# VectorE's and ScalarE's work on the quads as a loop with waits on registers, and PSUM banks of its own for the last quad

## The chip, the cores and the metric

The kernel runs on one core of a Trainium2 chip. The core has five engines, each with its own instruction stream: TensorE (PE in the profile), VectorE (DVE), ScalarE (ACT), GpSimd (POOL) and SyncE (SP), which issues most of the loads. They meet only at semaphores. The metric is the device time of one execution in microseconds, the median of several runs. All times below are in microseconds unless marked otherwise.

## What is computed

Attention for one new token of each of 32 sequences, over the last 512 positions of the key and value caches, with 32 query heads that share 8 key/value heads, and a projection on either side:

```python
B, Sq, D = 32, 1, 512
Hq, Hkv, Sk, Dh = 32, 8, 2048, 128
W = 512                                  # the window: the last 512 positions
q = (x @ wq).reshape(B, Sq, Hq, Dh).transpose(0, 2, 1, 3)
k = jnp.repeat(k_cache[:, :, Sk - W:, :], 4, axis=1)
v = jnp.repeat(v_cache[:, :, Sk - W:, :], 4, axis=1)
scores = jnp.einsum("bhqd,bhkd->bhqk", q, k) * (Dh ** -0.5)
p = softmax(scores, axis=-1)
o = jnp.einsum("bhqk,bhkd->bhqd", p, v)
out = o.transpose(0, 2, 1, 3).reshape(B, Sq, Hq * Dh) @ wo
```

Everything is bfloat16. The two windows are 33.5 MB each, wq and wo 4 MB each, so some 75.5 MB have to come from memory.

## The kernel before

**Quads.** The 32 sequences are worked on in eight quads of four, q = 0 to 7. The keys of a quad are one load K(q) of 4 MB (a partition holds 128 positions of one sequence, head and quarter of the window), its values one load V(q) of 4 MB, from quad 5 on in two pieces V(q).0 and V(q).1. There are two buffers for keys and two for values, used in turn. wo comes last, in three pieces W0 to W2, into the first key buffer.

**The steps of a quad**, with the letter that stands for each in the hand-written orders:

- T(q).0, T(q).1: VectorE transposes one half of the quad's keys each (line 516).
- S(q).0, S(q).1: TensorE multiplies each half with the queries, into the PSUM bank S_ps (line 346).
- M(q): VectorE takes the row maxima and their negative (lines 522 and 524).
- X(q): ScalarE's exponential, which also sums (line 565).
- N(q): VectorE's reciprocal and product, the weights in bfloat16 (lines 528 and 530).
- E(q): TensorE moves the weights to the rows on which the values lie, into EP_ps (line 360).
- G(q): ScalarE copies them out of PSUM into PTc (line 572).
- B(q): the weights are spread over a block-diagonal operand bd, heads 0 to 3 by VectorE (line 536), 4 to 7 by ScalarE (line 578).
- P(q): TensorE's weighted sum of the values, 32 groups of four products (line 372), into the four banks O_ps; P(q).a.b is groups a to b.
- C(q): the four pieces of the sum are copied to SBUF, by VectorE (line 541), ScalarE (line 583) or both.
- F(q): TensorE folds them into the layout that the output product wants (line 382), into F_ps; D(q): ScalarE stores the fold in o_sel (line 586).

After the last D, TensorE multiplies o_sel with wo (line 467), VectorE and ScalarE copy the result out (lines 550 and 597), and two stores end the kernel.

**What sets the order.** Every engine executes its instructions in the order in which they stand. TensorE's order is a head, three passes of a hardware loop over two quads (BODY_OPS), and a tail. VectorE's and ScalarE's orders are hand-written lists of all eight quads, DVE_OPS and ACT_OPS, without a loop; in VectorE's list the transposes of quads 6 and 7 stand ahead of steps of the quads before. `needs` gives what each step waits for, and ends in waits on constants. SP issues the loads in the order of LOADS: K(q) waits for T(q-2).1, V(q) for P(q-2) or the part of it that frees the piece, W0 to W2 for T6.1. A load that waits holds back all that stand behind it.

**PSUM.** The eight banks are S_ps, EP_ps, four of O_ps, F_ps and Y_ps (the output product). P(q) waits for the copies C(q-1), as all quads use the same four banks.

**Before the quads.** x is transposed by products, multiplied with wq into all eight banks (line 334), copied to SBUF in pieces of 512 columns by VectorE (line 505) and ScalarE (line 559) in turn, and the queries are transposed (line 508).

The loads, the orders and the loop's waits in the code:

```python
LOADS = """
K0 K1 V0.0 K2 V1.0 K3 V2.0 K4 V3.0 K5 K6 V4.0 K7 V5.0 V5.1 V6.0 V6.1 V7.0 V7.1 W0 W1 W2
""".split()
V_PIECES = 5 * [[0, 32]] + 2 * [[0, 16, 32]] + [[0, 18, 32]]
```

Of the kernel before, what the change touches and what calls it, by code (L numbers as in the profile page):

```python
# [19 lines left out]
S0.0 S0.1 S1.0 S1.1 E0 E1 P0.0.32  # L20
# [6 lines left out]
P7.0.18 P7.18.32 F6 F7  # L27
"""
ROUNDS = 3
DVE_OPS = """  # L30
T0.0 T0.1 T1.0 M0 T1.1 N0 M1 N1 B0.0.4 B1.0.4 T2.0 T2.1 M2 N2 B2.0.4 T3.0 T3.1 M3 N3 B3.0.4 T4.0
T4.1 M4 N4 B4.0.4 T5.0 C3.2.3 T5.1 C3.3.4 T6.0 M5 T6.1 N5 B5.0.4 C4.2.4 M6 T7.0 N6 T7.1 B6.0.4
C5.2.4 M7 N7 B7.0.5 C6.2.4 C7.2.4
"""
ACT_OPS = """
X0 X1 G0 B0.4.8 G1 B1.4.8 C0.0.4 X2 D0 G2 B2.4.8 C1.0.4 X3 D1 G3 B3.4.8 C2.0.4 X4 D2 G4 B4.4.8
C3.0.2 X5 D3 G5 B5.4.8 C4.0.2 X6 D4 G6 B6.4.8 C5.0.2 X7 D5 G7 B7.5.8 C6.0.2 C7.0.2 D6 D7
"""
# [14 lines left out]
def bass_standalone__sliding_block_cached__sampling_kernel(  # L53
# [22 lines left out]
    NG = 4  # L76
# [7 lines left out]
    orders = {"PE": head + sum(rounds, []) + tail, "DVE": ops_of(DVE_OPS), "ACT": ops_of(ACT_OPS)}  # L84

    ends, total = {}, {}
    for eng, ops in orders.items():
        for op in ops:
            kind = op[0]
            key = ("ANY", "C") if kind == "C" else (eng, kind)  # L90
            total[key] = total.get(key, 0) + (op[3] - op[2] if kind == "C" else 1)
            if kind == "C":
                ends["C", op[1]] = key + (4 * op[1] + 4,)
            elif kind == "B":
                for i in range(op[2], op[3]):
                    ends[kind, op[1], i] = key + (total[key],)
            elif kind == "P":
                for g in range(op[2], op[3]):
                    ends["P", op[1], g] = key + (total[key],)
            elif kind == "D":  # L100
                ends[op] = key + (total[key] + 1,)
            else:
                ends[op] = key + (total[key],)

    def needs(op):
# [3 lines left out]
        if kind == "T":  # L109
            d = [("S", q - 1, op[2])]  # L110
        elif kind == "S":
            d = [("T", q, op[2]), ("X", q - 1)]
        elif kind == "M":
            d = [("S", q, 1)]
        elif kind == "X":
            d = [("M", q), ("N", q - 1)]
        elif kind == "N":
            d = [("X", q), ("E", q - 1)]
        elif kind == "E":
            d = [("N", q), ("G", q - 1)]  # L120
        elif kind == "G":
            d = [("E", q)] + spread(q - NG)
        elif kind == "B":
            d = [("G", q), ("P", q - 2, 31)]
        elif kind == "P":
            d = spread(q) + [("C", q - 1)]
        elif kind == "C":
            d = [("P", q, 31), ("F", q - 2)]
        elif kind == "F":
            d = [("C", q)]  # L130
        elif kind == "D":
            d = [("F", q)]
        return [ends[n] for n in d if n[1] >= 0]

    with ExitStack() as es:
# [3 lines left out]
        K_sb = [sb(f"K_sb{i}", [P, R * DH], BF16) for i in range(2)]  # L139
# [9 lines left out]
        PTc = sb("PTc", [P, NG, R, REP], BF16)  # L149
        C_sb = sb("C_sb", [P, 2, 4, DH], F32)  # L150
        o_sel = sb("o_sel", [P, NI, B], BF16)
# [3 lines left out]
        maxv = sb("maxv", [P, NQ], F32)  # L155
        negmax = sb("negmax", [P, NQ], F32)
        sums = sb("sums", [P, NQ], F32)
        recip = sb("recip", [P, NQ], F32)
# [10 lines left out]
        F_id = spare[:, 1280:1536].bitcast(F32).rearrange("p (r h) -> p r h", r=4)  # L169
        m_id = spare[:, 1536:1792].bitcast(F32).rearrange("p (b h k) -> p b h k", b=4, h=HKV)  # L170
        F_hd = spare[:, 1792:1856].bitcast(F32)
        m_red = spare[:, 1856:1920].bitcast(F32)
# [7 lines left out]
        S_ps, EP_ps, O_ps, F_ps, Y_ps = ps[:, 0], ps[:, 1], ps[:, 2:6], ps[:, 6], ps[:, 7]  # L180

        def folds(q):
            return (F_ps if q < NQ - 1 else S_ps)[:, 0:4 * NI]
# [57 lines left out]
        def _(sp):  # L241
# [3 lines left out]
            for op in ops_of(" ".join(LOADS)):  # L245
                kind, q = op[0], op[1]
                if kind == "K":
                    if q >= 2:
# [23 lines left out]
        def _(pool):  # L272
# [10 lines left out]
            pool.sem_inc(op_sem["ACT", "D"], 1)  # L283
# [3 lines left out]
            diag(F_id[:, :, :], [[-32, 4], [-1, HQ]], "pool_f")  # L287
            diag(m_id[:, :, :, :], [[-32, 4], [-4, HKV], [-1, KB]], "pool_m")
# [30 lines left out]
        def _(pe):  # L319
# [48 lines left out]
            def pv(q, g0, g1):  # L368
                for g in range(g0, g1):
                    for b in range(4):  # L370
                        pr = slice(32 * b, 32 * b + 32)
                        ins = pe.matmul(  # L372
                            O_ps[:, b, :],
# [6 lines left out]
            def fold(q):  # L380
                for d in range(4):
# [3 lines left out]
                        rhs=C_sb[:, q % 2, :, NI * d:NI * d + NI],  # L385
# [11 lines left out]
            def waits_of(op):  # L397
# [3 lines left out]
                if kind == "S" and op[2] == 0:  # L401
                    yield ("ONE", "pool_qbd"), 4 * (q // 2) + 4
                    if q == 0:
                        yield ("ONE", "dve_q"), 4
                        yield ("ONE", "act_q"), 4
                elif kind == "E" and q == 0:
                    yield ("ONE", "pool_e"), 2
                elif kind == "F" and q < NQ - 1:
# [51 lines left out]
            for j, (i0, i1) in enumerate(WOP):  # L460
                pe.wait_ge(sem_wo[j], 16)
                last = j == len(WOP) - 1
                for cs in ((0, 1), (2, 3)) if last else (range(4),):
                    for i in range(i0, i1):
                        for c in cs:
# [3 lines left out]
                                lhsT=o_sel[:, i, :],  # L469
# [6 lines left out]
        def spread_args(q, h):  # L476
            return bd[:, q % 2, :, h, :], PTc[:, q % NG], mask[:, h:h + 1]

        def pick_args(q, r):
            pr = slice(32 * r, 32 * r + 32)  # L480
            return C_sb[pr, q % 2], O_ps[pr, :, r * DH:(r + 1) * DH]

        @block.vector
        def _(dve):
            wait = Waits(dve)
# [5 lines left out]
            dve.tensor_reduce(  # L491
                F_hd[:, :], F_id[:, :, :].rearrange("p r h -> p h r"), AX.X, ALU.add
            ).then_inc(s["dve_c"], 1)
            dve.wait_ge(s["pool_m"], 2)
            dve.tensor_reduce(
                m_red[:, :].rearrange("p (h k) -> p h k", h=HKV),
                m_id[:, :, :, :].rearrange("p b h k -> p h k b"), AX.X, ALU.add,
            ).then_inc(s["dve_c"], 1)
            dve.wait_ge(s["dve_c"], 2)
            dve.tensor_reduce(  # L500
                mask[:, :], m_red[:, :].rearrange("p (h k) -> p h k", h=HKV), AX.X, ALU.add
            ).then_inc(s["dve_c"], 1)
            for n in range(4):
                dve.wait_ge(s["pe_q"], 2 * n + 1)
                dve.tensor_copy(Q_row[:, 1024 * n:1024 * n + 512], ps[:, 2 * n]).then_inc(s["dve_q"], 1)  # L505
            dve.wait_ge(s["dve_q"], 4)
            dve.wait_ge(s["act_q"], 4)
# [6 lines left out]
            def turn(q, w):  # L514
                dve.wait_ge(sem_k[q % 2], 16 * (q // 2 + 1))
                return dve.transpose(  # L516
                    KT_sb[:, w].bitcast(F32).rearrange("p r c t -> p r (c t)"),
                    K_sb[q % 2][:, :].bitcast(F32).rearrange("p (r w c) -> p r w c", r=R, w=2)[:, :, w],
                )

            def maxes(q):
                dve.tensor_reduce(maxv[:, q:q + 1], S_ps, AX.X, ALU.max).then_inc(s["dve_m"], 1)  # L522
                dve.wait_ge(s["dve_m"], q + 1)
                return dve.tensor_scalar(  # L524
                    negmax[:, q:q + 1], maxv[:, q:q + 1], -SCALE, None, op0=ALU.mult)

            def norm(q):
                dve.reciprocal(recip[:, q:q + 1], sums[:, q:q + 1]).then_inc(s["dve_r"], 1)
                dve.wait_ge(s["dve_r"], q + 1)
                return dve.tensor_scalar(  # L530
                    P_bf[:, :], P_f32[:, :], recip[:, q:q + 1], None, op0=ALU.mult)

            def spread(q, h0, h1):
                for h in range(h0, h1):
                    o, i, m = spread_args(q, h)
                    ins = dve.tensor_scalar(o, i, m, None, op0=ALU.mult)  # L536
                return ins

            def pick(q, r0, r1):
                for r in range(r0, r1):  # L540
# [89 lines left out]
```

## Time and profile before

| | us |
|---|---|
| median of 3 runs (183.39 to 183.97) | 183.55 |
| the profiled execution | 183.87 |
| its span, first to last instruction | 182.6 |
| TensorE busy | 118.9 (65%) |
| VectorE busy | 105.8 (58%) |
| ScalarE busy | 49.7 (27%) |
| GpSimd busy | 12.4 (7%) |
| 16 transposes of keys on VectorE, 4.43 each | 70.5 |
| moved: 75.70 MB, mean 415 GB/s | |

The page cuts the span into 40 slices of 4.6 us and gives the busy share of each engine and of the 16 DMA engines in tenths; PEclk is the clock that TensorE was granted, in tenths of full speed (mean 0.822). The chain is followed back from the last instruction, at each step to what released it. A timeline lists instructions in order of time: start, duration, engine, line, operation, what it writes and reads, and how often, and in brackets the idle time before it with what ended it. An engine whose idle time nobody waits for costs nothing.

### The profile page before, as it was taken

Reading aid. Unit: us, or ns where it says so; the run is one execution under the profiler, and the core shown is the slowest. Engines: PE = TensorE matmul, PEld = TensorE weight load, DVE = VectorE, ACT = ScalarE, POOL = GpSimd, SP = SyncE. Lnnn points to the kernel's source line nnn. Section 1 sums busy time; section 2 is a strip of 40 time slices with the busy share of each in tenths; the row PEclk is TensorE's granted clock in tenths of the full one; section 3 lists DMA queues with packets and bytes.
Section 4 is the critical chain, followed back from the end, with each engine's and each line's share of the span. In section 5 each row is a group of like instructions: output and inputs, shape, how many; then the busy total and the mean of one; then the engine's idle time right before and its main releaser. Section 6 shows DMA issues by size and latency. Waiting matters only on the chain.

```text
span 182.6 us, 3659 instructions
## 1 busy us (share of the span) xinstructions
PE 118.9 (65%) x1636; PEld 57.6 (32%) x1636; DVE 105.8 (58%) x101; ACT 49.7 (27%) x92; POOL 12.4 (7%) x34
## 2 busy tenths in 40 slices
PE   0029901425869898049954899334299869996984
PEld 0013300101535353015521453003035434552553
DVE  0031499999559713983279317999902799633030
ACT  3001300000490527402470107100106406443031
POOL 7400012000300000003000000003000000000000
PEclk9999995555769999756995589755559999999999
DMA  6999999999999999999999999999999999999991
GB/s 235 461 431 409 424 459 438 431 395 460 449 431 388 449 456 416 395 452 449 425 398 438 438 447 409 431 438 445 424 416 416 427 424 438 416 436 437 424 374 56
DMA packets 3461, 75.70 MB, mean 415 GB/s; under 512 B 412, under 2 KB 508, under 8 KB 636
## 3 DMA queue, kind: packets, MB, share of 16 engines
q1 hardware_dynamic: 3360, 75.52, 96.7%
q8 instruction: 7, 0.11, 0.3%
q10 hardware_dynamic: 92, 0.05, 0.1%
q14 instruction: 2, 0.02, 0.0%
HBM read 75.53 MB, written 0.03 MB: 414 GB/s over the span
## 4 chain that ended last, share of the span: by engine, by line
DMA 39%; PE 28%; DVE 25%; ACT 3%; issue 3%; SPq 0%; DVEq 0%
DVE KT_sb L516 20%; DMA K_sb<-in_k_cache_dram 16%; DMA V_sb<-in_v_cache_dram 16%; PE ps L372 16%; DMA V_sb<-in_wq_dram 7%; PE ps L334 5%; PE ps L346 3%; DVE QT_sb L508 2%; PE ps L360 2%; ACT bd L578 1%; PE ps L382 1%; DVE C_sb L541 1%; PE ps L467 1%; DVE maxv L522 1%; DVE bd L536 1%
## 5 line engine op out<-in xcount | busy, mean ns | idle before, releaser
L516 DVE STREAM_TRANSPOSE KT_sb<-K_sb 128x4096 f32<-128x4096 f32 x16 | 70.5, 4429 | 4.6 <-DMA K_sb<-in_k_cache_dram 4.5
L372 PE MATMUL ps<-V_sb,bd 32*128 32x512 bf16 x1024 | 62.7, 398 | 9.6 <-DMA V_sb<-in_v_cache_dram 6.5
L346 PE MATMUL ps<-KT_sb,QBD 128*32 128x512 bf16 x256 | 24.6, 527 | 36.2 <-DVE KT_sb L516 32.1
L372 PEld LDWEIGHTS ps<-V_sb,bd 32*128 32x128 bf16 x1024 | 27.0, 97 | 40.5 <-issue 9.8
L346 PEld LDWEIGHTS ps<-KT_sb,QBD 128*32 128x32 bf16 x256 | 6.6, 113 | 52.4 <-DVE KT_sb L516 35.4
L536 DVE TENSOR_SCALAR bd<-PTc,mask 128x512 bf16<-128x512 bf16 x33 | 9.4, 349 | 22.5 <-ACT PTc L572 22.5
L565 ACT ACTIVATE P_f<-ps,negmax 128x512 f32<-128x512 f32 x8 | 5.5, 689 | 58.0 <-DVE negmax L524 58.0
L578 ACT ACTIVATE bd<-PTc,mask 128x512 bf16<-128x512 bf16 x31 | 19.9, 712 | 0.3
L583 ACT ACTIVATE C_sb<-ps 32x512 f32<-32x512 f32 x22 | 13.0, 589 | 21.7 <-PE ps L372 21.4
L541 DVE COPY C_sb<-ps 32x512 f32<-32x512 f32 x10 | 6.9, 693 | 12.9 <-PE ps L372 12.7
L312 POOL COPY QBD<-QT_sb 32x256 bf16<-32x256 bf16 x16 | 6.3, 396 | 106.0 <-PE ps L346 91.2
L572 ACT ACTIVATE PTc<-ps 128x512 bf16<-128x512 f32 x8 | 4.8, 595 | 27.9 <-PE ps L360 27.9
L382 PE MATMUL ps<-C_sb,F_pad 128*128 128x128 f32 x64 | 12.0, 345 | 0.4 <-DVE C_sb L541 0.4
L382 PEld LDWEIGHTS ps<-C_sb,F_pad 128*128 128x128 f32 x64 | 10.2, 242 | 4.8 <-issue 2.9
L360 PE MATMUL ps<-P_bf,E_sb 128*128 128x128 bf16 x128 | 9.5, 233 | 2.2 <-DVE P_bf L530 2.2
L334 PE MATMUL ps<-V_sb,bd 128*128 128x512 bf16 x32 | 9.2, 459 | 1.9 <-DMA V_sb<-in_wq_dram 1.9
L360 PEld LDWEIGHTS ps<-P_bf,E_sb 128*128 128x128 bf16 x128 | 8.1, 105 | 6.3 <-issue 3.4
L522 DVE TENSOR_REDUCE maxv<-ps 128x1 f32<-128x512 f32 x8 | 5.5, 687 | 7.5 <-PE ps L346 7.5
L323 PE MATMUL ps<-bd 32*128 32x128 bf16 x4 | 0.6, 294 | 10.6 <-DMA bd<-in_x_dram 10.6
L487 DVE CAST bd<-ps 128x512 bf16<-128x512 f32 x1 | 0.7, 691 | 11.3 <-PE ps L323 11.3
L559 ACT ACTIVATE KT_sb<-ps 128x512 bf16<-128x512 f32 x4 | 2.4, 598 | 17.1 <-PE ps L334 17.1
L505 DVE CAST KT_sb<-ps 128x512 bf16<-128x512 f32 x4 | 2.8, 692 | 6.7 <-PE ps L334 6.7
(29 smaller groups left out, 31.0 us busy)
## 6 DMA issues: line engine op xcount, KB each, us to landing
K_sb<-in_k_cache_dram SPq DMA_DIRECT2D x8, 4096.0 KB, 24.6
V_sb<-in_v_cache_dram SPq DMA_DIRECT2D x5, 4096.0 KB, 29.4
V_sb<-in_v_cache_dram SPq DMA_DIRECT2D x4, 2048.0 KB, 21.0
V_sb<-in_wq_dram SPq DMA_DIRECT2D x1, 4096.0 KB, 12.3
K_sb<-in_wo_dram SPq DMA_DIRECT2D x1, 2816.0 KB, 20.9
V_sb<-in_v_cache_dram SPq DMA_DIRECT2D x1, 2304.0 KB, 13.1
V_sb<-in_v_cache_dram SPq DMA_DIRECT2D x1, 1792.0 KB, 14.8
K_sb<-in_wo_dram SPq DMA_DIRECT2D x1, 1024.0 KB, 22.7
```

Source lines behind the costliest of these rows:

```text
L312: pool.tensor_copy(QBD[pr].rearrange("p u a (h c) -> p u a h c", h=HKV).rearrange("p u (w t) h c -> p (u w) t h c", w=2)[:, :, :, :, 4 * b ...
L334: ins = pe.matmul(ps[:, n], lhsT=xT_sb[:, kt, :], rhs=wq_sb[:, kt, n * 512:(n + 1) * 512], start=kt == 0, stop=kt == DKT - 1, tile_positio ...
L346: ins = pe.matmul(S_ps[32 * c:32 * c + 32, :], lhsT=QBD[:, q % 2, 2 * w + t, c0:c0 + 32], rhs=KT_sb[:, w, :, KB * h:KB * h + KB, t], start ...
L360: ins = pe.matmul(EP_ps[:, e * R:(e + 1) * R], lhsT=window[:, KB - 1 - k:KB - 1 - k + P], rhs=P_bf[:, k * R:(k + 1) * R], start=k == 0, st ...
L372: ins = pe.matmul(O_ps[:, b, :], lhsT=bd[pr, q % 2, 4 * g:4 * g + 4].rearrange("p r h e -> p (r h e)"), rhs=V_sb[q % 2][pr, 512 * g:512 * ...
L382: ins = pe.matmul(folds(q), lhsT=F_sb[:, d].rearrange("p h d -> p (h d)"), rhs=C_sb[:, q % 2, :, NI * d:NI * d + NI], start=d == 0, stop=d ...
L516: return dve.transpose(KT_sb[:, w].bitcast(F32).rearrange("p r c t -> p r (c t)"), K_sb[q % 2][:, :].bitcast(F32).rearrange("p (r w c) -> ...
L522: dve.tensor_reduce(maxv[:, q:q + 1], S_ps, AX.X, ALU.max).then_inc(s["dve_m"], 1)
L536: ins = dve.tensor_scalar(o, i, m, None, op0=ALU.mult)
L541: dve.tensor_copy(*pick_args(q, r)).then_inc(op_sem["ANY", "C"], 1)
L578: ins = act.activation(o, i, ACTF.Copy, scale=m)
L583: act.activation(*pick_args(q, r), ACTF.Copy).then_inc(op_sem["ANY", "C"], 1)
```

## The change

The lists DVE_OPS and ACT_OPS go. VectorE's and ScalarE's steps are hardware loops over n = 0 to 7. VectorE's turn n is T(n).0, T(n).1, then (from n = 2) its half of C(n-2), then M(n), N(n), B(n); ScalarE's is X(n), then (from n = 2) D(n-2), then G(n), its half of B(n), then (from n = 1) its half of C(n-1). What is left over of quads 6 and 7 stands behind the loops. Semaphore levels that depend on n are computed into registers; a branch on n being odd chooses the key buffer. SP increments some semaphores ahead of K2 by constants (BIAS), so that levels are a multiple of n plus a positive number.

TensorE keeps its loop and its body; its head now has E0 ahead of S1, and P0 in four pieces with E1 between them; its tail has P7 in four pieces. All PSUM banks are renumbered, and P(7) goes to the four upper banks (those of S_ps, EP_ps, F_ps and Y_ps), so it waits for D(5) instead of C(6); F(6) and F(7) go to the two lowest banks. C_sb has one buffer for quads 0 to 6 and one for quad 7. PTc and the small statistics have one buffer instead of four or eight. The queries are copied in two pieces of 1024 columns per engine instead of four of 512, and the mask is reduced in one step instead of two. The order of the loads and what they wait for is unchanged.

```diff
 HEAD_OPS = """
-S0.0 S0.1 S1.0 S1.1 E0 E1 P0.0.32
+S0.0 S0.1 E0 S1.0 S1.1 P0.0.12 E1 P0.12.16 P0.16.20 P0.20.32
 """
 TAIL_OPS = """
-P7.0.18 P7.18.32 F6 F7
+P7.0.12 P7.12.16 P7.16.18 P7.18.32 F6 F7
 """
-DVE_OPS = """
-T0.0 T0.1 T1.0 M0 T1.1 N0 M1 N1 B0.0.4 B1.0.4 T2.0 T2.1 M2 N2 B2.0.4 T3.0 T3.1 M3 N3 B3.0.4 T4.0
-T4.1 M4 N4 B4.0.4 T5.0 C3.2.3 T5.1 C3.3.4 T6.0 M5 T6.1 N5 B5.0.4 C4.2.4 M6 T7.0 N6 T7.1 B6.0.4
-C5.2.4 M7 N7 B7.0.5 C6.2.4 C7.2.4
-"""
-ACT_OPS = """
-X0 X1 G0 B0.4.8 G1 B1.4.8 C0.0.4 X2 D0 G2 B2.4.8 C1.0.4 X3 D1 G3 B3.4.8 C2.0.4 X4 D2 G4 B4.4.8
-C3.0.2 X5 D3 G5 B5.4.8 C4.0.2 X6 D4 G6 B6.4.8 C5.0.2 X7 D5 G7 B7.5.8 C6.0.2 C7.0.2 D6 D7
-"""
...
         elif kind == "P":
-            d = spread(q) + [("C", q - 1)]
+            d = spread(q) + [("C", q - 1) if q < LAST else ("D", q - 2)]
...
-        PTc = sb("PTc", [P, NG, R, REP], BF16)
+        PTc = sb("PTc", [P, R, REP], BF16)
...
-        S_ps, EP_ps, O_ps, F_ps, Y_ps = ps[:, 0], ps[:, 1], ps[:, 2:6], ps[:, 6], ps[:, 7]
+        O_ps, S_ps, EP_ps, F_ps, Y_ps = ps[:, 0:4], ps[:, 4], ps[:, 5], ps[:, 6], ps[:, 7]
 
         def folds(q):
-            return (F_ps if q < NQ - 1 else S_ps)[:, 0:4 * NI]
+            return (F_ps if q < LAST - 1 else O_ps[:, q - LAST + 1])[:, 0:4 * NI]
+
+        def sums_of(b, q):
+            return ps[:, b if q < LAST else 4 + b]
...
+                    if q == 2:
+                        for key, n in BIAS.items():
+                            sp.sem_inc(op_sem[key], n)
...
-            for n in range(4):
-                dve.wait_ge(s["pe_q"], 2 * n + 1)
-                dve.tensor_copy(Q_row[:, 1024 * n:1024 * n + 512], ps[:, 2 * n]).then_inc(s["dve_q"], 1)
+            for n in range(2):
+                dve.wait_ge(s["pe_q"], 4 * n + 2)
+                dve.tensor_copy(
+                    Q_row[:, 2048 * n:2048 * n + 1024], ps[:, 4 * n:4 * n + 2].rearrange("p b n -> p (b n)")
+                ).then_inc(s["dve_q"], 1)
...
+            with dve.Fori(0, NQ) as n:
+                odd = dve.snap(n % 2)
+                one = dve.snap(n + 1)
+                pieces = dve.snap(PIECES * n + 1)
+                landed = dve.snap(16 * (n // 2) + 16)
+                turned = [dve.snap(2 * n + w + 1) for w in range(2)]
+
+                def turn(i):
+                    dve.wait_ge(sem_k[i], landed)
+                    for w in range(2):
+                        dve.wait_ge(op_sem["PE", "S"], turned[w])
+                        dve.transpose(
+                            KT_sb[:, w].bitcast(F32).rearrange("p r c t -> p r (c t)"),
+                            K_sb[i].bitcast(F32).rearrange(
+                                "p (r w c) -> p r w c", r=R, w=2)[:, :, w],
+                        ).then_inc(done("T"), 1)
+
+                with dve.If(odd):
+                    turn(1)
+                with dve.Else():
+                    turn(0)
+                with dve.If(n > 1):
+                    dve.wait_ge(op_sem["PE", "P"], pieces)
+                    for r in (2, 3):
+                        dve.tensor_copy(*pick_args(r)).then_inc(op_sem["ANY", "C"], 1)
+                dve.wait_ge(op_sem["PE", "S"], 2 * n + 4)
+                dve.tensor_reduce(maxv[:, :], S_ps, AX.X, ALU.max).then_inc(s["dve_m"], 1)
+                dve.wait_ge(s["dve_m"], one)
+                dve.tensor_scalar(
+                    negmax[:, :], maxv[:, :], -SCALE, None, op0=ALU.mult
+                ).then_inc(done("M"), 1)
+                dve.wait_ge(op_sem["ACT", "X"], one)
+                dve.reciprocal(recip[:, :], sums[:, :]).then_inc(s["dve_r"], 1)
+                dve.wait_ge(op_sem["PE", "E"], one)
+                dve.wait_ge(s["dve_r"], one)
+                dve.tensor_scalar(
+                    P_bf[:, :], P_f32[:, :], recip[:, :], None, op0=ALU.mult
+                ).then_inc(done("N"), 1)
+                dve.wait_ge(op_sem["ACT", "G"], one)
+                for h in range(4):
+                    ins = dve.tensor_scalar(
+                        bd[:, bass.ds(odd, 1), :, h, :].rearrange("p o r e -> p (o r) e"),
+                        PTc[:, :, :], mask[:, h:h + 1], None, op0=ALU.mult)
+                ins.then_inc(done("B"), 1)
+            for last in range(2):
+                dve.wait_ge(op_sem["PE", "P"], ends["P", LAST - 1 + last, R // 4 - 1][2])
+                for r in (2, 3):
+                    dve.tensor_copy(*pick_args(r, last)).then_inc(op_sem["ANY", "CL"[last]], 1)
...
+            with act.Fori(0, NQ) as n:
+                odd = act.snap(n % 2)
+                one = act.snap(n + 1)
+                act.wait_ge(op_sem["DVE", "M"], one)
+                act.activation(
                     P_f32[:, :].rearrange("p (k r) -> p k r", k=KB),
                     S_ps.rearrange("p (r k) -> p k r", k=KB), ACTF.Exp,
-                    bias=negmax[:, q:q + 1], scale=SCALE, accum_out=sums[:, q:q + 1],
-                )
...
+                    bias=negmax[:, :], scale=SCALE, accum_out=sums[:, :],
+                ).then_inc(done("X"), 1)
+                with act.If(n > 1):
+                    act.wait_ge(op_sem["PE", "F"], one)
+                    folded(bass.ds(4 * n, 4), 0).then_inc(done("D"), 1)
+                act.wait_ge(op_sem["PE", "E"], n + 2)
+                act.activation(
+                    PTc[:, :, :], EP_ps.rearrange("p (e r) -> p r e", e=REP), ACTF.Copy
+                ).then_inc(done("G"), 1)
+                act.wait_ge(done("G"), one)
+                for h in range(4, HKV):
+                    ins = act.activation(
+                        bd[:, bass.ds(odd, 1), :, h, :].rearrange("p o r e -> p (o r) e"),
+                        PTc[:, :, :], ACTF.Copy, scale=mask[:, h:h + 1])
+                ins.then_inc(done("B"), 1)
+                with act.If(n > 0):
+                    act.wait_ge(op_sem["PE", "P"], PIECES * n + PIECES + 1)
+                    for r in (0, 1):
+                        act.activation(*pick_args(r), ACTF.Copy).then_inc(op_sem["ANY", "C"], 1)
...
```

## The prediction

> **What bounds the kernel now.** I read the slices first, then the chain, then the instructions in order of time. Letters: T turns a quad's keys (two VectorE transposes), S scores, M maxima, X exponential, N normalising, E and G move the weights to the value rows, B spreads them, P weighted sum, C copies it out of PSUM, F folds, D stores the fold; n and q count the quads.
>
> ```profile
> PEclk9999995555769999756995589755559999999999
> DMA  6999999999999999999999999999999999999991
> DMA 39%; PE 28%; DVE 25%; ACT 3%; issue 3%; SPq 0%; DVEq 0%
> ```
>
> The DMA engines are full from the second slice to the last but one. 75.5 MB pass one queue, a 4 MB load every 9.75 us (K4 lands at 92.3, V3 at 102.0). The last piece, W2, issued at 157.2 and 22.9 long, lands at 180.1, and the last product ends at 180.4 of a span of 182.6. So two bounds coincide at the end: the stream, and the chain through the last quads. What matters is whether work runs ahead of the stream or is held back by itself.
>
> ```profile
> 72.65 8.77 DVE L516 STREAM_TRANSPOSE KT_sb<-K_sb 128x4096 f32<-128x4096 f32 x2 [2.80 <-DMA K_sb<-in_k_cache_dram]
> 83.42 0.69 DVE L522 TENSOR_REDUCE maxv<-ps 128x1 f32<-128x512 f32 x1 [2.01 <-PE ps L346]
> 85.35 0.49 DVE L530 TENSOR_SCALAR P_bf<-P_f,recip 128x512 bf16<-128x512 f32 x1
> 89.96 1.15 DVE L536 TENSOR_SCALAR bd<-PTc,mask 128x512 bf16<-128x512 bf16 x4 [4.13 <-ACT PTc L572]
> 92.28 8.77 DVE L516 STREAM_TRANSPOSE KT_sb<-K_sb 128x4096 f32<-128x4096 f32 x2 [1.18 <-DMA K_sb<-in_k_cache_dram]
> ...
> 122.12 4.45 DVE L516 STREAM_TRANSPOSE KT_sb<-K_sb 128x4096 f32<-128x4096 f32 x1
> 126.59 0.69 DVE L522 TENSOR_REDUCE maxv<-ps 128x1 f32<-128x512 f32 x1
> 127.39 4.43 DVE L516 STREAM_TRANSPOSE KT_sb<-K_sb 128x4096 f32<-128x4096 f32 x1
> 138.40 1.14 DVE L536 TENSOR_SCALAR bd<-PTc,mask 128x512 bf16<-128x512 bf16 x4 [6.00 <-ACT PTc L572]
> ```
>
> VectorE's own timeline: start, duration, and in brackets the idle time before. Quad 3 (72.65 to 91.11) already has the order of the new loop: T, M, N, B, one after another, 18.46 us; quad 4 (92.28 to 111.16) takes 18.88. Afterwards the old list runs ahead: both transposes of quad 6 (122.12, 127.39) lie before the B of quad 5 (138.40), in time in which that B waits. With quad 7's transposes done by 154.20, the old kernel makes up the wait for V4, which lands only at 131.1.
>
> ```profile
> 81.47 1.90 PE L346 MATMUL ps<-KT_sb,QBD 128*32 128x512 bf16 x16 [2.43 <-DVE KT_sb L516]
> 83.30 2.08 PE L382 MATMUL ps<-C_sb,F_pad 128*128 128x128 f32 x8
> 85.31 2.99 PE L372 MATMUL ps<-V_sb,bd 32*128 32x512 bf16 x48
> 88.23 1.07 PE L360 MATMUL ps<-P_bf,E_sb 128*128 128x128 bf16 x16
> 89.23 4.49 PE L372 MATMUL ps<-V_sb,bd 32*128 32x512 bf16 x80
> ...
> 168.18 7.09 PE L372 MATMUL ps<-V_sb,bd 32*128 32x512 bf16 x128 [1.72 <-DVE C_sb L541]
> ```
>
> TensorE in the same quad 3: S3.1, F1, the first 12 groups of P2, E3, the rest of P2. E3 stands behind F1 and P2, so they are on VectorE's path to B. The last line is P7, which waited 1.72 us for the copy of quad 6.
>
> **The serial loop.** The new VectorE program has T(n+1) behind B(n) for every n. B(n) waits for G(n), which waits for E(n), F(n-2) and part of P(n-1); what queues behind that wait is T(n+1), so S(n+1) and the load of K(n+3), which needs T(n+1)'s buffer. One turn of the loop is therefore the length of quads 3 and 4, 18.46 and 18.88, mean 18.67, plus the turn itself. Term by term from the end of T, in quad 3: S's second half and its signal 2.00, F 2.01 less the 0.12 by which TensorE is ahead of the maxima, P 2.92, E 1.0, G 0.1+0.63, B 1.15, together 9.69, behind 8.77 of T.
>
> C's two VectorE copies (1.42 by the pair at 142.21) now stand between T and M in each turn and cost nothing: VectorE idles 2.01 there for S. Without that cover they would cost 1.42 a turn. M, X, N (2.42) lie beside F and P (4.9). On ScalarE, D and the conditional lie in its 3.64 us of idle time before G; its C copies (1.20) end long before the next X. Weights buffered once instead of four times hold nothing up: G(n) comes after E(n), which comes after N(n), itself behind B(n-1).
>
> **The turn.** The trace has no loop on VectorE. Register values, the branch back, the branch on odd quads: from below 0, since four B instructions (1.15) can cover them and TensorE, looping already, starts S4.0 just 0.13 after its transpose at 96.73, against 0.05 for S4.1 inside the body; from above 0.84, the longest issue gap that TensorE shows (ahead of F). I take 0.25, nearer the looping row. [...] Handoffs whose semaphore level is in a register I price at nothing: TensorE's loop has such waits and starts 0.05 after its releaser.
>
> **The start.** The copies of the queries become two of 1024 columns per engine. ScalarE's last one starts at 22.40 as before, its bank coming last; 128 columns take 0.273, 512 take 0.598, so 1024 some 1.03 instead of 0.61: +0.4. Loop entry with nothing to hide it: 0 to 1.5 (two gaps of the longest kind), taken as 0.6. Reductions on the masks end before the queries come, and SP's five semaphore increments stand ahead of K2, which waits for T0 anyway: nothing for either. T0: 26.76 + 1.0 = 27.8 to 36.5. Quad 0 has neither F nor P before E: 2.00 + 2.42 + E at the low clock 1.71 + 0.1 + 0.63 + 1.15 = 8.0, B0 ends at 44.5. Quad 1 has P but no F: turn 0.25 + 8.77 + (9.69 - 2.01 and 10.11 - 2.01, mean 7.9), B1 ends at 61.4.
>
> **The end.** Six further turns of 18.67 + 0.25 = 113.5: B7 ends at 174.9, the rest of P6 2.6 later (91.11 to 93.72 in quad 3) at 177.5; before it was 166.47. P7 now writes the four upper banks and needs no copy of quad 6 first: it starts at once, gaining the 1.7, and takes 7.1, to 184.6. From there to the end as before, 182.6 - 175.27 = 7.3: the copies of quad 7, its fold and store, the output product, the result. **Span 191.9.** The profiled run was 183.87 for a span of 182.6, the median 183.55, 0.95 over the span; so the time is 191.9 + 0.95 = **192.8 us**.
>
> **The loads.** Would the stream starve? SP issues in order, and from issue to the first data takes about 2.5 (12.29 for the first 4 MB less 9.75). K6 goes out at T4's end, 99.5 + 8.8 = 108.3, and must by 111.7 - 2.5 = 109.2; K7 at 127.2, by 131.1 - 2.5 = 128.6; before, they had 8 us more. V2 to V5 have more room than that. A starved microsecond costs nothing, as W2 at 180.1 is needed at about 189. V4 (131.1) is wanted at about 131: no wait of note. So the bound moves from the stream to the serial loop.
>
> **Rivals.**
> (a) The clock stays up: no change or a trifle faster. Quad 2, at full clock, took 16.46 (53.38 to 69.84). Six turns of 16.46 + 0.25 end B7 at 161.7 and the chain at 178.7, under the stream; W2 at 180.1 and the 2.3 after it give a span of 182.4 and a time of 183.4. The place is the gap from P(n-1)'s end to S(n)'s second half; it decides if the clock doesn't drop there. In the rows it changes at steps of about 3.4 us, and dropped when TensorE was busy for 1.0 to 1.2 of such a stretch (113.1 to 116.5), not at 2.0 (147.1 to 150.5). The new gap is 2 idle, 1.05 of S, 3.35 idle: nearly every such stretch falls below. Chance 0.05, with another 0.05 for half the turns at full clock: turns of 17.6, 185.5.
> (b) The turn is dear: the branch back waits for code. The profile has 7 packets of 0.11 MB of instructions, 16 KB each; the only transfers of 16 KB timed are the stores, 1.4 and 1.8 us, so seven turns would add 10 to 13: 202 to 205. Against: VectorE's list is about 100 instructions in all, the loop a fraction, and TensorE's far longer loop shows no such gap. Chance 0.10. [...]
> (c) P7's 1.7 us counts and the rest hides, because the loop doesn't hold T back. The stream still ends at 180.1, so the floor is a span of 182.3, and only a stream running a little faster gives more than 0.3%. VectorE executes in order, which speaks against it: 0.02.
>
> **How the numbers follow.** Forecast 0.78; (a) 0.05 and its half 0.05; (b) 0.10; (c) 0.02. Within the forecast: no turn cost, entry 0.1 and turns of 18.2 (clock up earlier) give 187.8; turns of 18.88 + 0.84, entry 1.5 and quad 1 at the low clock give 199.5. The range is 187.5 to 200; what lies outside is the chances of the rivals. A difference of 0.3%, 0.55 us, is about what can be told from none. Faster 0.03, same 0.05, slower 0.92.
>
> **What would show it.** Right: VectorE's T(n+1) starts under 0.5 us after B(n), each time 18.5 to 19.2 us after T(n) from quad 2 on; K4 to K7 waited for by nobody, the DMA engines idle for some us late in the span; the clock low at each second half of S; P7 directly behind P6 and ending near 184.6; the chain nearly all VectorE and TensorE. Wrong: T(n+1) waiting for K loads (then the stream still rules), gaps of over 1 us ahead of T (turn cost), or S's halves taking 1.05 us each (clock).

## The result and the profile after

The changed kernel takes 195.3 us (median of 4 runs, 193.65 to 197.41) against 183.6 for the kernel before; the ratio is 1.055, with a 95% interval of 1.052 to 1.058. The interval leaves out the two longest of the four runs, 196.8 and 197.4; five more runs of the same kernel gave 193.6 to 195.6 and a ratio of 1.058 (1.055 to 1.061). The profiled execution took 193.84 with a span of 192.4.

The slices and the chain of the changed kernel's page:

```profile
PEclk9999985555559966995599579966995899579999
DMA  6999999999999999999999799999999999999400
PE 37%; DVE 21%; issue 18%; DMA 18%; ACT 3%; DVEq 2%; SPq 0%; ACTq 0%
```

The DMA engines are idle in the last two slices and busy for four tenths of the one before: the stream has ended (W2 lands at 180.9 instead of 180.1) while the kernel goes on to 192.4. DMA holds 18% of the chain instead of 39%, TensorE 37% instead of 28%, VectorE 21% instead of 25%. The 18% under "issue" are no idle time: four fifths of it lie in the first transposes of the turns (63.04 to 67.14, for instance, while T2.0 runs from 62.77), so that VectorE's part is rather some 35%. Of DMA's 18%, 6% are the load of wq at the start and 11% the one load of V4, through which the chain passes (110.03 to 131.76). VectorE's timeline (start, duration, operation, idle time before):

```profile
100.64 8.77 DVE L510 STREAM_TRANSPOSE KT_sb<-K_sb 128x4096 f32<-128x4096 f32 x2
117.72 1.14 DVE L539 TENSOR_SCALAR bd<-PTc,mask 128x512 bf16 x4 [3.82 <-ACT PTc L582]
118.88 8.77 DVE L510 STREAM_TRANSPOSE KT_sb<-K_sb 128x4096 f32<-128x4096 f32 x2
137.12 1.14 DVE L539 TENSOR_SCALAR bd<-PTc,mask 128x512 bf16 x4 [4.99 <-ACT PTc L582]
138.40 8.77 DVE L510 STREAM_TRANSPOSE KT_sb<-K_sb 128x4096 f32<-128x4096 f32 x2
...
156.53 8.77 DVE L510 STREAM_TRANSPOSE KT_sb<-K_sb 128x4096 f32<-128x4096 f32 x2
```

Each T(n+1) starts right behind B(n): 117.72 + 1.14 = 118.86, then 118.88. No K load is waited for any more. Quad 6's transposes start at 138.40, where before they started at 122.12 and 127.39, and from quad 2 on VectorE sits idle for 3.7 to 5.0 us of each turn ahead of B, waiting for G. TensorE's timeline, P4's first part and the end:

```profile
131.76 3.57 PE L363 MATMUL ps<-V_sb,bd 32*128 32x512 bf16 x48 [0.16 <-DMA V_sb<-in_v_cache_dram]
...
169.19 3.63 PE L363 MATMUL ps<-V_sb,bd 32*128 32x512 bf16 x48
172.76 1.07 PE L351 MATMUL ps<-P_bf,E_sb 128*128 128x128 bf16 x16
173.76 11.40 PE L363 MATMUL ps<-V_sb,bd 32*128 32x512 bf16 x208
```

The last line is the rest of P6 and all of P7 in one, without the 1.72 us between them that the kernel before had. The gain is there, but the rest of P6 starts at 173.76, where before it started at 161.97. The first line will matter below: P4 waits 0.16 us for V4.

### The profile page after: what moved, and what is told of

Same layout as the page of the kernel before. It is cut to its first block, busy times and chain, and to the rows that moved or that the text cites. A ratio compares the mean times of both kernels' runs of the same rounds, so it can differ in the third digit from the quotient of the medians.

```text
span 192.4 us, 3853 instructions
## 1 busy us (share of the span) xinstructions
PE 121.7 (63%) x1636; PEld 58.5 (30%) x1636; DVE 109.8 (57%) x103; ACT 46.9 (24%) x85; POOL 12.6 (7%) x34
## 4 chain that ended last, share of the span: by engine, by line
PE 37%; DVE 21%; issue 18%; DMA 18%; ACT 3%; DVEq 2%; SPq 0%; ACTq 0%
PE ps L363 16%; DVE KT_sb L510 16%; DMA V_sb<-in_v_cache_dram 11%; DMA V_sb<-in_wq_dram 6%; PE ps L337 6%; PE ps L325 5%; PE ps L373 5%; PE ps L351 4%; ACT PTc L582 2%; DVE QT_sb L490 2%; DVE bd L539 1%; PE ps L458 1%; DVE C_sb L546 1%; ACT KT_sb L556 1%; DVEq L507 0%
## 5 line engine op out<-in xcount | busy, mean ns | idle before, releaser
L363 PE MATMUL ps<-V_sb,bd 32*128 32x512 bf16 x1024 | 61.7, 393 | 0.2 <-DMA V_sb<-in_v_cache_dram 0.2
L337 PE MATMUL ps<-KT_sb,QBD 128*32 128x512 bf16 x256 | 26.3, 550 | 52.3 <-DVE KT_sb L510 52.3
L363 PEld LDWEIGHTS ps<-V_sb,bd 32*128 32x128 bf16 x1024 | 25.8, 97 | 32.0 <-issue 6.8
L539 DVE TENSOR_SCALAR bd<-PTc,mask 128x512 bf16 x32 | 9.1, 350 | 32.3 <-ACT PTc L582 32.3
L587 ACT ACTIVATE bd<-PTc,mask 128x512 bf16 x32 | 20.5, 710 | 1.4 <-ACT PTc L582 1.4
L373 PE MATMUL ps<-C_sb,F_pad 128*128 128x128 f32 x64 | 14.4, 396 | 0.4 <-DVE C_sb L546 0.4
L373 PEld LDWEIGHTS ps<-C_sb,F_pad 128*128 128x128 f32 x64 | 12.5, 291 | 6.1 <-DVE C_sb L523 5.0
L594 ACT ACTIVATE C_sb<-ps 32x512 f32<-32x512 f32 x14 | 8.2, 587 | 7.9 <-PE ps L363 7.7
L523 DVE COPY C_sb<-ps 32x512 f32<-32x512 f32 x12 | 8.3, 693 | 0.4
L546 DVE COPY C_sb<-ps 32x512 f32<-32x512 f32 x4 | 2.8, 693 | 8.1 <-PE ps L363 8.0
L485 DVE CAST KT_sb<-ps 128x1024 bf16<-128x1024 f32 x2 | 2.4, 1224 | 7.1 <-PE ps L325 7.1
## 6 DMA issues: line engine op xcount, KB each, us to landing
K_sb<-in_k_cache_dram SPq DMA_DIRECT2D x8, 4096.0 KB, 19.5
K_sb<-in_wo_dram SPq DMA_DIRECT2D x1, 2816.0 KB, 18.1
```

The source lines that it names most:

```text
L337: ins = pe.matmul(S_ps[32 * c:32 * c + 32, :], lhsT=QBD[:, q % 2, 2 * w + t, c0:c0 + 32], rhs=KT_sb[:, w, :, KB * h:KB * h + KB, t], start ...
L363: ins = pe.matmul(sums_of(b, q), lhsT=bd[pr, q % 2, 4 * g:4 * g + 4].rearrange("p r h e -> p (r h e)"), rhs=V_sb[q % 2][pr, 512 * g:512 * ...
L373: ins = pe.matmul(folds(q), lhsT=F_sb[:, d].rearrange("p h d -> p (h d)"), rhs=C_sb[:, q // LAST, :, NI * d:NI * d + NI], start=d == 0, st ...
L523: dve.tensor_copy(*pick_args(r)).then_inc(op_sem["ANY", "C"], 1)
L539: ins = dve.tensor_scalar(bd[:, bass.ds(odd, 1), :, h, :].rearrange("p o r e -> p (o r) e"), PTc[:, :, :], mask[:, h:h + 1], None, op0=ALU ...
L587: ins = act.activation(bd[:, bass.ds(odd, 1), :, h, :].rearrange("p o r e -> p (o r) e"), PTc[:, :, :], ACTF.Copy, scale=mask[:, h:h + 1])
```

## The experiments

**1. The loops written out.** Same instructions, same order, constants in the waits and in the addresses of bd and o_sel (ScalarE's loop likewise):

```diff
-            with dve.Fori(0, NQ) as n:
-                odd = dve.snap(n % 2)
-                one = dve.snap(n + 1)
+            for n in range(NQ):
+                odd = n % 2
+                one = n + 1
...
-                with dve.If(odd):
-                    turn(1)
-                with dve.Else():
-                    turn(0)
+                turn(odd)
```

> The changed kernel with VectorE's and ScalarE's loops written out in full: the same instructions in the same order, with waits on constants. Theory (the serial order costs the time, the loop itself hardly anything): at most what the trace shows of the turn goes, 0.02 to 0.13 between B(n) and T(n+1) and about 0.12 more from G to B than before, eight times each, so 191.8 to 194 us against 193.7. Rival (registers, branches and their fetches cost the time): back to 183 to 186 us.

Measured: 192.1 us (191.4 to 194.3), ratio 1.044 (1.042 to 1.045), a span of 190.9. VectorE's timeline of this kernel, B6 and T7, then ScalarE's, G7 and B7, and last the same two of the changed kernel:

```profile
155.17 1.14 DVE L536 TENSOR_SCALAR bd<-PTc,mask 128x512 bf16<-128x512 bf16 x4 [4.45 <-ACT PTc L579]
156.22 8.77 DVE L510 STREAM_TRANSPOSE KT_sb<-K_sb 128x4096 f32<-128x4096 f32 x2
...
172.52 0.60 ACT L579 ACTIVATE PTc<-ps 128x512 bf16<-128x512 f32 x1 [3.42 <-PE ps L351]
173.15 2.56 ACT L584 ACTIVATE bd<-PTc,mask 128x512 bf16<-128x512 bf16 x4
...
173.86 0.60 ACT L582 ACTIVATE PTc<-ps 128x512 bf16<-128x512 f32 x1 [4.20 <-PE ps L351]
174.64 2.56 ACT L587 ACTIVATE bd<-PTc,mask 128x512 bf16 x4 [0.18 <-ACT PTc L582]
```

T7 begins 0.09 before the last B instruction is over, where the loop had it 0.02 to 0.13 after; and from G's end to B are 0.03, where the loop took 0.18 on ScalarE (174.46 to 174.64) and 0.15 on VectorE: some 0.25 to 0.35 a turn. The waits on registers are not what costs this. M, X and G wait for levels in registers too, and in both kernels they start 0.05, 0.04 and 0.04 after what released them; later in the loop are B and D (0.13 instead of 0.04 behind F), the ones that write to an address worked out from n. No run changes the addresses alone.

The time differs by 1.5 us of span between the two profiled executions, and by 2.1 to 2.6 us going by the ratios (1.2% to 1.4% of 183.6). That bounds the loop's own cost, it doesn't measure it: T7 starts only 0.31 earlier than in the changed kernel, as P4 waits 0.95 for V4 here and the time saved before is lost there, and 0.86 of the 1.5 is the first part of P6, which this execution ran in 2.77 instead of 3.63, at a higher clock (PEclk on its page 8 in the slice from 167.0; in the changed kernel 7 in the one from 168.4, and 0.75 while that part runs). So the loop itself is the smaller part, at most about a quarter of the loss; the order keeps the rest.

**2. The old lists with the last quad's own banks.** The kernel before, in which only this is changed (with the banks renumbered for it, and a semaphore of its own for C7):

```diff
-            d = spread(q) + [("C", q - 1)]
+            d = spread(q) + [("C", q - 1) if q < NQ - 1 else ("D", q - 2)]
...
+        def sums_of(b, q):
+            return ps[:, b if q < NQ - 1 else 4 + b]
...
-                            O_ps[:, b, :],
+                            sums_of(b, q),
```

> The kernel before with nothing of the change but the last quad's PSUM banks: P7 doesn't wait for C6. Theory (before, the stream of loads ends the kernel together with the chain): P7 starts 1.7 earlier and the product waits for W2 instead, which lands at about 180.1, so a span of 182.3 to 182.6 and 183.2 to 183.6 us, no difference that can be told. Rival (P7's wait was on the path alone): 1.7 us less, 181.9 us.

Measured: 183.57 us, ratio 1.0001 (0.9992 to 1.001). TensorE's timeline of it:

```profile
165.85 7.40 PE L375 MATMUL ps<-V_sb,bd 32*128 32x512 bf16 x128 [0.69 <-DMA V_sb<-in_v_cache_dram]
...
176.85 1.41 PE L470 MATMUL ps<-K_sb,o_sel 128*32 128x128 bf16 x88 [0.91 <-DMA K_sb<-in_wo_dram]
179.23 0.93 PE L470 MATMUL ps<-K_sb,o_sel 128*32 128x128 bf16 x40 [0.96 <-DMA K_sb<-in_wo_dram]
```

P7 no longer waits for a copy but for V7, and the output product waits twice for wo. The 1.7 us turn into waits for the stream.

**3. The loop with shared banks.** The changed kernel, whose last quad uses the same banks as the others, with P7 waiting for C6 (and the folds of quads 6 and 7 in the banks of S_ps and EP_ps):

```diff
-            d = spread(q) + [("C", q - 1) if q < LAST else ("D", q - 2)]
+            d = spread(q) + [("C", q - 1)]
...
-            return ps[:, b if q < LAST else 4 + b]
+            return ps[:, b]
```

> The changed kernel with the last quad in the same four PSUM banks as the others, so that P7 waits for C6 again. Theory (in the changed kernel the chain alone ends late, the stream 8 us before it): P7 waits 1.7 us behind P6 and all of it shows, 195.2 to 195.6 us against 193.7. Rival (the wait hides as it would in the kernel before): 193.7 us.

Measured: 195.5 us (194.6 to 198.4), ratio 1.064 (1.060 to 1.068). TensorE's timeline:

```profile
172.89 4.50 PE L363 MATMUL ps<-V_sb,bd 32*128 32x512 bf16 x80
179.11 7.09 PE L363 MATMUL ps<-V_sb,bd 32*128 32x512 bf16 x128 [1.72 <-DVE C_sb L546]
```

The wait of 1.72 is back, and nothing behind it absorbs it: from T7's start to the end are 37.9 us, in the changed kernel 35.9. In time the ratios differ by 0.6% to 0.9%, 1 to 1.6 us; the spread of these kernels is too wide to tell that from 1.7. The banks are worth something only where the chain, not the stream, ends the kernel.

**4. The loop with T(n+1) ahead of B(n).** Loops and register waits stay; VectorE's turn is reordered, C(n-1) moving behind B(n) as well (the comments behind # are added here):

```diff
+            turn(0, 16, (1, 2))
+            with dve.Fori(0, LAST) as n:
...
+                scale_row(n, one)          # M(n), N(n)
+                with dve.If(odd):
+                    turn(0, landed, turned)   # T(n+1)
+                with dve.Else():
+                    turn(1, landed, turned)
+                spread(odd, one)           # B(n)
+                with dve.If(n > 0):
+                    dve.wait_ge(op_sem["PE", "P"], pieces)   # C(n-1)
...
+            scale_row(LAST, LAST + 1)
+            spread(LAST % 2, LAST + 1)
```

> The changed kernel with its loops and register waits, VectorE's turn reordered: M(n), N(n), T(n+1).0, T(n+1).1, B(n), C(n-1); T(0) stands ahead of the loop, M, N and B of quad 7 behind it. Theory (T(n+1) behind B(n) is the cost): a turn without waits is about 14 us, under the 19.5 of the stream, so the stream ends the kernel again: K loads waited for, W2 landing at about 180, a span of 182.2 to 183.5 and 183.0 to 184.5 us. Rival (the loop itself costs): 190 us or more.

Measured: 183.65 us, ratio 1.0006 (0.9997 to 1.0015). VectorE's timeline:

```profile
111.53 8.77 DVE L503 STREAM_TRANSPOSE KT_sb<-K_sb 128x4096 f32<-128x4096 f32 x2 [5.71 <-DMA K_sb<-in_k_cache_dram]
...
125.25 8.77 DVE L503 STREAM_TRANSPOSE KT_sb<-K_sb 128x4096 f32<-128x4096 f32 x2
138.32 1.14 DVE L527 TENSOR_SCALAR bd<-PTc,mask 128x512 bf16 x4 [4.30 <-ACT PTc L590]
```

K loads are waited for again, 5.71 us at T5, and T6 (125.25 to 134.0) lies ahead of B5 (138.32). With the loop kept, the loss is gone: the order was its cause. This version equals the kernel before and doesn't beat it, as both end on the stream (here the output product waits 0.78 for the last of wo).

**5. The old lists, serial only at the end.** To see which turns count, the transposes of quads 6 and 7 are moved in the kernel before, behind B5 and B6:

```diff
-T4.1 M4 N4 B4.0.4 T5.0 C3.2.3 T5.1 C3.3.4 T6.0 M5 T6.1 N5 B5.0.4 C4.2.4 M6 T7.0 N6 T7.1 B6.0.4
-C5.2.4 M7 N7 B7.0.5 C6.2.4 C7.2.4
+T4.1 M4 N4 B4.0.4 T5.0 C3.2.3 T5.1 C3.3.4 M5 N5 B5.0.4 T6.0 T6.1 C4.2.4 M6 N6 B6.0.4
+T7.0 T7.1 C5.2.4 M7 N7 B7.0.5 C6.2.4 C7.2.4
```

> The kernel before with its straight lists, in which the transposes of quad 6 stand behind B5 and those of quad 7 behind B6; all else, the early quads and the PSUM banks too, as before. Theory (two serial turns behind the arrival of V4 at 131.1 make the loss, and the serial turns of the early quads nothing of it): B5 ends at about 139.5, two turns of 18.2 to 19.5 follow, P6 ends near 179 and P7 waits its 1.7, so 194 to 197 us. Rival (each serial turn adds its share, so that two of seven cost some 3 us): 186 to 188 us.

Measured: 196.2 us (194.0 to 196.8), ratio 1.067 (1.061 to 1.072). VectorE's and TensorE's timelines, and last P4's first part in the kernel before:

```profile
137.90 1.14 DVE L536 TENSOR_SCALAR bd<-PTc,mask 128x512 bf16<-128x512 bf16 x4 [12.37 <-ACT PTc L572]
138.95 8.77 DVE L516 STREAM_TRANSPOSE KT_sb<-K_sb 128x4096 f32<-128x4096 f32 x2
...
130.92 5.31 PE L372 MATMUL ps<-V_sb,bd 32*128 32x512 bf16 x48 [5.85 <-DMA V_sb<-in_v_cache_dram]
...
131.15 5.31 PE L372 MATMUL ps<-V_sb,bd 32*128 32x512 bf16 x48 [5.83 <-DMA V_sb<-in_v_cache_dram]
```

Quad 5 is early here (VectorE idles 12.37 us ahead of B5), yet T6 starts at 138.95, half a microsecond later than in the changed kernel. TensorE waits 5.85 us for V4, which stands behind K6 in the queue, and all that follows hangs on it. The kernel before has the same wait and the same slow first part of P4; what differs is the two turns behind it.

**6. The changed order, running ahead only at the end.** The kernel of experiment 1, in which T6 and T7 move to between N and B of the quad before; quads 0 to 5 stay serial:

```diff
-                turn(odd)
+                if n < LAST - 1:
+                    turn(n)
...
+                if n in (LAST - 2, LAST - 1):
+                    turn(n + 1)
                 dve.wait_ge(op_sem["ACT", "G"], one)
```

> The written-out version of the changed kernel's order, in which only the transposes of quads 6 and 7 are moved, to between N and B of the quad before. The early quads stay serial. Theory: the late start of the early quads is lost in the slack of the loads and the end runs ahead again; the stream ends the kernel, at most 1 us late from K6 and K7 issued late, 183.4 to 185 us. Rival (each serial turn adds its share): five of seven turns remain, 189 to 191 us.

Measured: 183.7 us (183.5 to 184.6), ratio 1.002 (0.999 to 1.004). VectorE's timeline:

```profile
130.00 8.76 DVE L508 STREAM_TRANSPOSE KT_sb<-K_sb 128x4096 f32<-128x4096 f32 x2
138.69 1.10 DVE L537 TENSOR_SCALAR bd<-PTc,mask 128x512 bf16<-128x512 bf16 x4
```

The early quads are still late (T5 starts at 116.84, in the kernel before at 111.72), T6 fits into the wait for V4 and E5, T7 (143.67) starts ahead of B6 (152.35), and the stream ends the kernel: the output product waits 0.76 and 0.96 for wo. Experiments 5 and 6 together: two serial turns at the end are enough for the whole loss, and the serial turns before them cost nothing without these two.

**7. The clock kept up.** The changed kernel with products into the bank of the output product, still unused then, ahead of both halves of S in TensorE's loop; they add work and nobody reads them:

```diff
+            def keep_warm(count):
+                flat = E_sb[:, :, :, :].rearrange("p e m j -> p (e m j)")
+                for _ in range(count):
+                    pe.matmul(Y_ps, lhsT=flat[:, 0:P], rhs=flat[:, 0:512], start=True, stop=True,
+                              tile_position=(0, 0))
...
+                    if op[0] == "S":
+                        keep_warm((8, 12)[op[2]])
                     emit(op, waits)
```

> The changed kernel with 8 further products of 128x512 ahead of each S.0 and 12 ahead of each S.1 in TensorE's loop, into the bank of the output product, which nobody reads; they fill the gaps in which the clock falls. Theory (the clock is a part of the turn: 18.2 to 19.5 at the low clock, 16.5 at the full one): turns of 16.5 to 17 in quads 2 to 4; then quad 5 waits for V4 at about 131, B5 ends near 136.8, and two turns of 16.6 follow, 187 to 189 us. Rival (the clock adds nothing, or the further products hold S up): 193.5 us or more. A third reading (no wait for V4): 183.5 us.

Measured: 191.4 us (190.8 to 191.6), ratio 1.042 (1.040 to 1.044), mean clock 0.901 instead of 0.805. VectorE's and TensorE's timelines:

```profile
79.70 8.77 DVE L518 STREAM_TRANSPOSE KT_sb<-K_sb 128x4096 f32<-128x4096 f32 x2
96.90 8.77 DVE L518 STREAM_TRANSPOSE KT_sb<-K_sb 128x4096 f32<-128x4096 f32 x2
113.97 8.77 DVE L518 STREAM_TRANSPOSE KT_sb<-K_sb 128x4096 f32<-128x4096 f32 x2
139.66 8.77 DVE L518 STREAM_TRANSPOSE KT_sb<-K_sb 128x4096 f32<-128x4096 f32 x2
...
72.91 1.16 PE L373 MATMUL ps<-C_sb,F_pad 128*128 128x128 f32 x8 [0.40 <-DVE C_sb L531]
...
131.18 5.30 PE L363 MATMUL ps<-V_sb,bd 32*128 32x512 bf16 x48 [5.78 <-DMA V_sb<-in_v_cache_dram]
```

The turns shrink to 17.1 and 17.2, and what quads 2 to 4 gain goes into the wait for V4: quad 5 gets there 5.8 us early. No products had been put into that gap; PEclk on the page, 9 in every slice from 61.8 to 128.4, is 6 in the two from 128.4 to 137.9, and the first part of P4 took 5.30 instead of the 2.77 of the quads before. That is most of what the expectation missed: B5 ends at 139.5, not near 136.8. What the time gains against the changed kernel comes from the two shorter turns behind it.

**8. The same with V4 ahead of K6.**

```diff
-K0 K1 V0.0 K2 V1.0 K3 V2.0 K4 V3.0 K5 K6 V4.0 K7 V5.0 V5.1 V6.0 V6.1 V7.0 V7.1 W0 W1 W2
+K0 K1 V0.0 K2 V1.0 K3 V2.0 K4 V3.0 K5 V4.0 K6 K7 V5.0 V5.1 V6.0 V6.1 V7.0 V7.1 W0 W1 W2
```

> The one before with V4 loaded ahead of K6. Theory: V4 lands near 121.5 and K6 near 131; quad 5 no longer waits, T6 starts at about 131, turns of 16.6 end B7 near 164, and the stream ends the kernel, 183.2 to 185 us. Rival (the order of the two loads doesn't matter): as the one before.

Measured: 186.3 us (186.1 to 188.0), ratio 1.017 (1.013 to 1.021). The wait for V4 is gone and T6 starts at 131.91. But the next one takes its place, at quad 6, on TensorE's timeline:

```profile
145.69 2.77 PE L363 MATMUL ps<-V_sb,bd 32*128 32x512 bf16 x48 [2.35 <-DMA V_sb<-in_v_cache_dram]
```

That is P5's first part, waiting 2.35 us for V5.0 (in the kernel before it started at 145.77), with one serial turn behind it. By the ratios, about seven tenths of the loss are recovered, without a change in VectorE's order, by extra work on TensorE.

**9. V4 ahead of K6 alone**, without the further products: the same edit to the changed kernel.

> The changed kernel with V4 loaded ahead of K6, without further products. In the changed kernel the wait for V4 and the serial turns reach quad 5 at the same moment (P4 waits 0.16). Theory: without the wait for V4 the serial turns alone set T6, at 138 to 138.5, and nothing changes, 193 to 194.5 us in the shorter runs. Rival (the order of the loads is what the changed kernel loses on): 186 to 190 us.

Measured: 193.8 us (192.6 to 195.7), ratio 1.052 (1.049 to 1.055). TensorE's timeline, P4's first part:

```profile
131.67 3.69 PE L363 MATMUL ps<-V_sb,bd 32*128 32x512 bf16 x48
```

P4 starts at 131.67 without a wait and T6 at 138.43, both within 0.1 of the changed kernel. At this clock (mean 0.805 in both) the serial turns and V4 reach quad 5 together; removing one leaves the other.

**10. The changed kernel again.**

> The changed kernel once more, in more runs, beside the one before. Theory (turns of 18.2 and 19.5 alternate by where the clock's steps fall, and the steps fall differently in each execution): times spread from 193 to 198 us, more than the 0.5 us of the kernels that end on the stream. Rival (the first runs were disturbed): all within 0.6 us of 193.7.

Measured: 193.6, 193.8, 194.8, 194.8 and 195.6 us; the kernel before, measured beside it, spread by 0.5. The longest was the profiled one (span 194.2): its T0 started 0.84 later (28.68 against 27.84) and its T6 1.33 later (139.73 against 138.40). The expected mechanism is only in part what this execution shows. Its turns from quad 2 on alternate as before, each within 0.12 of the first profile's; the lateness is made ahead of them, 0.84 before T0, all of it there already when VectorE transposes the queries (24.35 against 23.51), and 0.31 in quad 1. A kernel that ends on the chain passes such delays on, where one that ends on the stream can hide them. The 197.4 of the first four runs did not come again; what made that run so long stays open.

## Why the prediction was right

**The bound.** Right: it moved from the stream to VectorE's serial loop, with T(n+1) directly behind B(n) and nobody waiting for K4 to K7. Experiment 4 shows it from the other side. Two of the signs named came only in part: the turns lie between 18.1 and 19.5, not 18.5 and 19.2, and the chain is not nearly all VectorE and TensorE, as it passes through the load of V4.

**The sum.** Span forecast 191.9, profiled 192.4. T0 at 27.8 (27.84 measured), B0's end 44.5 (44.97), B1's 61.4 (62.65), B7's 174.9 (175.75), P7's end 184.6 (185.16), the end as before 7.3 (7.2). The largest miss is quad 1: its first part of P took 4.08 at a granted clock of 0.67, more than either row it was priced from (2.99 at 0.92 and 3.40 at 0.81). The time forecast, 192.8, lies under the 195.3 measured, and under each of the nine runs. In the profiled execution 0.5 us of that is the span and 0.5 its distance to the time: the forecast took 0.95, a median less the span of another execution, whose own distance was 1.3, and here it is 1.44. The rest is the spread of the runs, of which the profiled one is among the shorter.

**The turn.** 18.67 + 0.25 = 18.92 forecast; from T2 (62.77) to T7 (156.53) 93.76 in five turns, 18.75. The single turns are 18.37, 19.50, 18.24, 19.52 and 18.13: the two rows of the kernel before, 18.46 and 18.88, did not show how far the clock can pull them apart (the first part of P took 2.77 at 1.00 in the first of these turns, 3.78 at 0.73 in the second). The cost of the loop, the author's choice between 0 and 0.84, was put at B's end (0.25) and at nothing in the handoffs; measured it is split between them, 0.01 to 0.14 at B's end and 0.12 from G to B (0.15 instead of 0.03), in sum near the 0.25. The waits on registers were rightly put at nothing; it is B, which writes to a computed address, that starts later. The 0.84 that bounded the turn from above was no gap in TensorE's work: it is idle time of the weight loads (PEld) ahead of F, while products run. It set nothing but the upper end of the range.

**Which turns count.** The prediction's sum was right and its account incomplete. It added up six turns from quad 2 on, and that path does set T6: with V4 out of the way it starts at the same time (experiment 9). But V4 was named only as "wanted at about 131: no wait of note", and there is a second path to the same moment: V4's landing alone makes T6 as late when the turns before it are early (experiment 5). Behind it, two serial turns are enough for the whole loss, and without them the serial turns before cost nothing (experiment 6). That the two paths meet at quad 5 within 0.2 us is luck; a shorter turn ahead of it would not by itself have given back the share that it has in the prediction's sum.

**What was hidden.** C's copies cost nothing, as forecast: from T's end to M are 2.00 in quad 1, without copies, and 2.01 in quad 3, with them. That holds at a clock of 0.50, as granted while S's second half ran in both; where experiment 7's page has PEclk at 9, F waits 0.40 for the copies in each turn. The stream starved a little: K6 was issued at 109.4 (forecast 108.3, limit 109.2), V4 landed 0.6 later than before, which quad 5 waited 0.16 for, and W2 0.8 later, which nobody waited for.

**The banks.** The wait of 1.7 us went as forecast and is back in experiment 3; in the times the difference is 1 to 1.6 us. Without the loop it would have been worth nothing, as rival (c) had it for the floor of the stream (experiment 2).

**The rivals.** (a), the full clock, was priced wrongly: 183.4 looked only at the stream's last byte. Experiment 7 reached turns of 17.1, which are the 16.46 with some 0.2 for the loop and the 0.40 that F waits for the copies, and 191.4, as V4 holds quad 5 and two turns follow. The 185.5 for half the turns is a span; as a time it would be some 186.4. (b), a wait for code at each turn, did not show: VectorE's seven turns show gaps of 0.01 to 0.14 and its entry 0.72, together 1.2 us, not 10 to 13, and the instructions are 7 packets of 0.11 MB as before.

## What to carry to other kernels

An instruction placed behind a wait waits too (T6, behind B5, started at 138.40, where before it started at 122.12): before rolling steps into a loop, look for what the old order had placed into the waits, and keep it ahead of them by working one step ahead in the loop (experiment 4 cost nothing). A stream that is always full says only when its last byte lands; look also for the load in the middle on which the last chain hangs, for what is saved ahead of its landing is lost in the wait for it (experiments 1 and 7). Where two paths reach a step together, shortening one of them gains nothing (experiment 9). And a wait removed from the chain is worth its length only if the chain, not the stream, ends the kernel.

## What the runs showed of the hardware

- The granted clock changes in steps: in the changed kernel's trace its stretches at one level, 0.50 or 1.00, the last one aside, last 6.83, 10.24, 13.65 or 30.72 us, in the kernel before 3.41, 10.24 or 20.48, all multiples of 3.413. Two turns (37.7 us) are nearly eleven steps (37.5), and long and short turns alternate; with the clock up from about 58 to 130 us (experiment 7, PEclk 9 in every slice from 61.8 to 128.4) the turns there differ by 0.13 only. In the kernel before it fell from 1.00 to 0.50 at 116.5, behind a stretch of 3.4 us (113.1 to 116.5) in which TensorE was busy for 0.96.
- Waits on a level in a register showed no cost of their own: M, X and G started 0.05, 0.04 and 0.04 us after what released them, in the loops and written out alike. Instructions that also write to an address worked out from n started later in the loops: B 0.15 (VectorE) and 0.18 (ScalarE) after G instead of 0.03, D 0.13 after F instead of 0.04. That the address is the reason is inferred from this contrast, not shown by a run of its own.
- A turn of VectorE's loop with a conditional in it showed 0.01 to 0.14 from B's end to T, alternating with the parity of n; written out, T starts 0.09 ahead of B's end. Entering the loop took 0.72 instead of 0.04.
- Filling TensorE's gaps with products that nobody reads raised the mean clock from 0.805 to 0.901 and shortened a turn by about 1.6 us.
